# A seventh buffer for the ring of kept sums, lent by the rounded masks, and a new order of issue

## The chip, the core and the metric

One NeuronCore of one Trainium2 chip. The metric is the device time of one execution in microseconds (us). PE is the engine of the matrix products, DVE, ACT and POOL are the three engines that work on elements, SP only issues transfers (DMAs).

## The reference, cut to what matters

```python
def _attn_ref(q, k, v):                      # q, k, v: (8, 8, 576, 64)
    scores = scale * np.matmul(q, k.transpose(0, 1, 3, 2))
    mask = (rel >= 0) & (rel < 64)           # rel = row position - column position
    ...                                      # softmax over the band
    return np.matmul(attn, v)

def _moe_ref(x, w_in, w_out):                # x: (4608, 512), w_in: (512, 2048), w_out: (2048, 512)
    h = x @ w_in
    g = np.where(h >= 1, h, np.where(h <= -1, 0.0, (h + 1) ** 2 / 4))
    return g @ w_out
```

Attention in a band of 64 keys comes first, and its output for each of the 4608 tokens is the input of a feed-forward layer.

## The kernel before, in words

**Stages.** The tokens go in nine tiles of 512. Three tiles are plain (`PLAIN = 3`): for each of 16 slices f of the hidden width, `ffn_in` (line 1218) makes h, a gate follows on ACT and DVE, and `ffn_out` (line 1258) adds to the output. Numbers are split into a high and a low part, and three products of the parts stand for one exact product. The six tiles left go in pairs, three "supers", by a scheme that does with seven block products what takes eight otherwise: sums and differences of the weights' blocks are made once, beside the plain stage (`add_sums`, line 938), and stored in HBM as `kept`; sums of the inputs are made on the chip. In each super, layer 1 (`ffn_product`, line 992, products on line 999) and layer 2 (`out_product`, line 1078, products on line 1085) run 56 products of six matmuls each.

**The ring.** Each of these products needs one block of kept sums, 256 KB, read from HBM by `ring_load` (line 976, transfer on line 979) into one of the ring's buffers. `add_ring` (line 981) makes 336 such loads in all. A load takes the next buffer in turn, and it is issued when the product that read that buffer last is done. The ring has six buffers: four are parts of the weight tile of slice 7, free once the last plain tile and the sums have used that slice, and two are buffers of the gates' parts `gh` and `gl`, free when the last plain tile's gates end. In the profile a buffer of the ring goes by the name of its tile, `wts`, `gh` or `gl`.

**Attention** runs in 36 steps of 128 tokens, spread over the whole as far as they go. From step 5 on, a step is: loads of q, k and twice v (lines 403, 407, 413), scores on PE (line 435), masked maximum and exponential, a 32x32 transpose on DVE (line 504), two stores to a scratch array `moved` in HBM (line 515), a read back in another order (line 530 or 533) into `ptd`, and then the product with v on PE (line 564). The read waits on SP until both stores have landed. The first steps (under 4) use masks that PE adds as a product with the unit matrix (line 428): `round_masks` (line 418) rounds the unit matrix and two masks into the tiles `idr` and `mskr`, 384 columns together, which nothing reads after that.

**Order.** Nothing is put in order by the compiler. `Plan` (line 134) holds every piece of work with a key, a cost for each engine that may do it, what it must come after and which buffers it takes and gives back; `Plan.run` (line 164) goes through a modelled time and puts out one piece after another, each on the engine that it chose. So all instructions of an engine and all transfers of SP's one queue stand in an order that the constants at the top of the file determine. The constants are keys and offsets (a unit is three quarters of the work of one slice on a plain tile), and `BACKLOG` is how far the modelled transfers may be behind before `run` lets SP issue another one. On the chip itself nothing waits for a key, a cost or `BACKLOG`: there only the order in each queue, and the semaphores of data and buffers, count.

**Start.** PE begins with matmuls on zeros (`warm`, line 291), which come before any loaded data: line 1422 gives the plan the cost of 8 but issues 13.

Of the kernel before, what the change touches and what calls it, by code (L numbers as in the profile page):

```python
# [11 lines left out]
F32R = mybir.dt.float32r  # L12
# [8 lines left out]
P = 128  # L21
QB = 64
SB = 2 * QB
WIN = 128
# [15 lines left out]
SOON = 5  # L40
JOIN = 8
BEHIND = 2
E_SPAN = -0.05
E_LEAD = 4.66
W_LEAD = -23.13
W_FIRST = (35.49, 50.06, 38.63, 36.68, -42.68)
W_STEP = 56.48
L_LEAD = 8.81
W_LATE = (-42.87, -19.84, -54.27, 11.82, -43.33)
V_LATE = 52.64  # L50
W0_KEY = -158.18
FIRST_LOAD = 0, (0,)
M_LATE = -3.69
W0_STEP = 28.15
FINE = 4
NWARM = 8
A_FIRST = (-130.89, -101.03, -86.53, -82.72)
A_NEXT = 21.89
A_STEP = 8.86
A_SPAN = 83.57  # L60
A_LEAD = -2.06
O_LAG = 3.31
BEGIN = dict(PE=1500, ACT=2300, DVE=2500, SP=2400)
PERIOD = 10240 / 3
HOP = dict(ACT=165, DVE=165, Pool=210, PE=210, SP=0)
# [5 lines left out]
EXP = 1545, 1440  # L71
S_PE = 1230, 1150
B_PE = 2210
B_DUE = (-1.9, -10.3, -2.66)
B_STEP = 16.55
B_FIRST = -49.18
A_END = -1.03
V_PE = 1270
NORM = dict(Pool=1300, DVE=610)
G_LATE = (6.24, 30.85, -58.26, 24.04, 0.27)  # L80
D_LATE = (10.58, -8.5, 39.35, -35.76, 47.54, 28)
TURN = 965, 100
HOP_SP = 660, 430
SLACK = 1000
V_PE_2 = 1290
SUM_PASS = 1900
SUM_KEEP = 430
V_LATE_2 = 63.45
P_LOAD = (-14.18, -18.03)
P_LOAD_V = (106.26, 73.14)  # L90
LAND = 800
WRITE = 1140
NOW = -2000
URGENT = 900
BACKLOG = 1487.14
MOVED = 3700
PATIENCE = dict(ACT=300, DVE=0, Pool=303, PE=0, SP=0)
BUFS = dict(qt=2, kt=2, vt=4, ps_a=2, sm=2, ptd=3, pt2=2, x=2, u=2, ps_h=2, a=2, gh=2, gl=2, acc=4, o=2, tmp=1)
BUFS.update({n: 1 for n in ("xtmp", "xs0", "xs1", "xs2", "xs3", "xs4", "xs5", "X", "Y")}, raw=4, ring=6, op=5)


PLAIN = 3
SUPERS = 3
H_STEP = 18.67
S_LATE = -18.48
S_PACE = 47.11
O_CHANGE = (18.66, -33.23, 40.4)
EARLY_2 = 13.35
A_SUPER = ((14.96, -42.48), (-9.45, -6.24))
P_SHIFT = ((-0.59, -6.76, -5.83, 5.27, -24.12), (2, 5.54, 6, 4.47, -26.37))  # L110
A_PAIR = ((6.06, 10.29), (3.01, 10.06))
P_DUE = 3.35
V_RUN = 1130, 930
S_RUN = 932, 954, 904
A_ORDER = (0, 4, 1, 5, 2, 6, 3, 7)
BUILD = (-11.57, 15.81)
X_SLOTS = 4, 0, 6, 1, 2, 3
G_FIRST = 8
RING_SLOT = 7
PARTS = (0, 0, 0), (1, 1, 1), (0, 5, 4), (1, 3, 2), (0, 4, 3), (1, 6, 5), (0, 2, 6)  # L120
WRITES = (1, None), (2, 1), (0, None), (3, 2), (3, 3), (1, 2), (2, 2)
R_LEAD = -5.21
R_LOAD = 370
L_DVE = 4, 6, 8
G_LEAD = (-39.31, 47.12, 21.92, 53.61)
OP_LEAD = 9.32
D_LEAD = 26.04


def packets(n, size, lead=2265):  # L130
# [3 lines left out]
class Plan:  # L134
# [10 lines left out]
    def add(self, key, cost, do, after=(), takes=(), gives=(), lag=0, shared=False, moves=None, behind=()):  # L145
        self.work.append((key, cost, do, set(after), takes, gives, lag, shared, moves, set(behind)))
        return len(self.work) - 1
# [85 lines left out]
def banded_attention_then_ffn(ctx: ExitStack, tc: tile.TileContext, q, k, v, w, masks, out, out_t, dims):  # L233
    nc = tc.nc
    B, H, S, D = dims
    NT, DM = B * S, H * D
# [7 lines left out]
    const = ctx.enter_context(tc.tile_pool(name="const", bufs=1))  # L244
# [17 lines left out]
    make_identity(nc, idt)  # L262
    msk = early[:, P:].rearrange("p (a n) -> p a n", n=WIN)
    nmsk = const.tile([P, 3, NEAR], F32, name="nmsk")
    idr = const.tile([P, P], F32R, name="idr")
    mskr = const.tile([P, 2, WIN], F32R, name="mskr")
    wpool = ctx.enter_context(tc.tile_pool(name="wpool", bufs=1))
    dram = ctx.enter_context(tc.tile_pool(name="dram", bufs=1, space=bass.MemoryType.DRAM))
    kept = [[dram.tile([P, 7, 2, 2, P], F32, name=f"kept{l}{n}") for n in range(NF // 2)] for l in range(2)]
# [21 lines left out]
    def warm(n):  # L291

        ps = bank("acc")
        for _ in range(n):
            nc.tensor.matmul(ps[:, :P], lhsT=ptd[0][:, 0], rhs=ptd[0][:, 0], start=True, stop=True)
# [4 lines left out]
    add = plan.add  # L300
# [14 lines left out]
    ws, wts, pairs, zs, us = {}, {}, {}, {}, {}  # L315
# [45 lines left out]
    def add_weights(f, units):  # L361
        g = f, units
        m = len(units) * DM
        act, high, join, low = 105 + .916 * m, 92 + .844 * m, 10 + 1.22 * m, 67 + 1.05 * m
        key = f * W_STEP - (W_FIRST[f] if f < len(W_FIRST) else W_LEAD) + .5 * units[0]
        x = add(W0_KEY + W0_STEP * (f + .5 * units[0]) if g != FIRST_LOAD else A_FIRST[0] - L_LEAD + .01, dict(SP=480 * (g != FIRST_LOAD)), lambda e: None if g == FIRST_LOAD else w_load(g), moves=packets(P, 8 * m))
        xr = add(key - W_LATE[0], dict(ACT=act), lambda e: w_rest(g), [x], takes=["u"])
        x = add(key - W_LATE[1], dict(ACT=act, DVE=67 + 1.05 * m), lambda e: w_top(g, e), [xr], shared=True)
        x = add(key - W_LATE[2], dict(DVE=join), lambda e: w_join(g), [x], shared=True)
        x = add(key - W_LATE[3], dict(ACT=high, DVE=30 + .6 * m), lambda e: w_high(g, e), [x], shared=True)  # L370
        x = add(key - W_LATE[4], dict(DVE=low, Pool=200 + 2.15 * m), lambda e: w_low(g, e), [x], gives=[("u", xr)], shared=True)
        for u in units:
# [207 lines left out]
    raws, xtmp, xops = {}, [], []  # L580
# [58 lines left out]
    early_values = []  # L639
# [13 lines left out]
    def freed(fs):  # L653
        return [x for f in fs for x in (l1[PLAIN - 1, f], l2[PLAIN - 1, f], *sums_read[0, f // 2], *sums_read[1, f // 2])]
# [27 lines left out]
    def add_turn(s, xs, dk, banks, sm):  # L682
        due = [dk + B_DUE[0], dk + B_DUE[0] + B_DUE[2]]
        x = [add(due[h], dict(DVE=LOWEST), lambda e, h=h: att_masked(s, h), [xs, last["m"]], gives=[banks[h]]) for h in range(2)]
        x = [add(due[h], dict(ACT=EXP[1]), lambda e, h=h: att_exp(s, h, False), [x[h]]) for h in range(2)]
        x = add(due[1], dict(DVE=430), lambda e: att_inverse(s, BOTH), x, shared=True)
        x = [add(due[1], dict(DVE=870, Pool=1650), lambda e: att_normalize(s, BOTH, e), [x], shared=True)]
        due = dk + B_DUE[1]
        if s == SOON:
# [76 lines left out]
    def add_step(t, i):  # L766
# [7 lines left out]
        if s < FIRST:  # L774
            key = due = A_FIRST[s]
        elif s >= JOIN:
            key = a_keys[s]
        else:
            key = a_keys[s]
            due = min(key + A_SPAN, soon(s))  # L780
        lk = key - L_LEAD
        apart = A_SUPER[t > PLAIN][1]
        if s == 0:
            last["r"] = add(lk, dict(ACT=480), lambda e: round_masks())
        if s == PE_STEPS - 2:
            last["m"] = add(lk + M_LATE, dict(SP=480), lambda e: load_masks(), moves=packets(P, 12 * NEAR))
        late = s >= JOIN
        vk, vc = lk + (V_LATE_2 if late else V_LATE), 450 if s < SOON else 640
        xq, xk, xv, xw = add_loads(s, lk, vk, vc)
# [25 lines left out]
        if s < SOON:  # L815
            for h in range(2):
                x = xs
                if not masked:
                    x = add(due + D_LATE[0], dict(DVE=MASKED[near(s)]), lambda e, h=h: att_masked(s, h), [x, last["m"]] if near(s) else [x], gives=[(ps, xs, h)])
                x = add(due + D_LATE[1], dict(DVE=800 if masked else MAXIMUM[near(s)]), lambda e, h=h: att_max(s, h, masked), [x])  # L820
                x = add(
# [26 lines left out]
        else:  # L848
            dk = key if s >= JOIN else min(key + E_SPAN, soon(s) - E_LEAD)
            x = add_turn(s, xs, dk, [(ps, xs, h) for h in range(2)], ("sm", xs))  # L850
            due = dk + B_DUE[1]
            first = taken = ready = [x]
# [85 lines left out]
    def add_sums(l, n):  # L938
# [4 lines left out]
        for c in range(2):  # L943
            k = key + c * S_PACE / 2
            xs = add(
# [18 lines left out]
    rings, ring_first, ring_slots = {}, [], {}  # L964

    def ring_slot(i):
        if i not in ring_slots:
            if i < 4:
                t = slot_tile(RING_SLOT)
                ring_slots.update({2 * a + b: t[:, a, b] for a in range(2) for b in range(2)})  # L970
            else:
                name = ("gh", "gl")[i - 4]
                ring_slots[i] = ffn.tile([P, DM], F32R, name=name, bufs=2, tag=name)
        return ring_slots[i]

# [4 lines left out]

    def add_ring(l, u, n, j, key):
        i, after = len(ring_first), [*sums_kept[l, n], *ring_first[-1:]]
        if i < 6:
            after += freed([RING_SLOT]) if i < 4 else [gates_end[0]]
        x = add(key - R_LEAD, dict(SP=R_LOAD), lambda e: ring_load(l, u, n, j, x), after, takes=["ring"], moves=packets(P, 4 * DM))
        if i < 6:
            ring_first.append(add(key - R_LEAD, dict(SP=0), lambda e: None, after))
        return x

# [226 lines left out]
    phs, gs, acc = {}, {}, {}  # L1216
# [59 lines left out]
    def out_late(t, q, i):  # L1276
        if t < PLAIN - 1 or q < NF - 2:
            return O_LAG
        return O_CHANGE[0] if q == NF - 2 else O_CHANGE[1 + i // 2]

# [27 lines left out]
    def soon(s):  # L1308

        t, i = s * SB // TMAX, s * SB % TMAX // SB  # L1310
        return step(t) + (FRONT * TMAX / 2 / 384 if 2 * i >= TMAX // SB else 0) - A_NEXT + i % 2

# [42 lines left out]
    def add_ffn(t):  # L1355
        first, before, x_out = {}, [x_in[t - 1]] if t else [], {}
        for f in range(NF):
            for r, key in parts(t, f):
# [9 lines left out]
                for i in subs(r):  # L1368
                    x_in[t, i] = xi
                xa, _, xh, xl = add_gate(t, f, r, key, G_LATE if t == 0 else [0] * 5, [xi], [("ps_h", xi)])  # L1370
                over = {x_out[i] for i in subs(r)} if f else set()
# [17 lines left out]
    gates_end = []  # L1389
# [26 lines left out]
    for t in reversed(range(PLAIN)):  # L1416
        for i in reversed(range(TILES[t] // SB)):
            at, apart = (step(t) - A_LEAD, A_STEP) if t < 2 else (step(t) - A_END - B_STEP - EARLY_2, B_FIRST)
            a_keys[starts[t] // SB + i] = key = min(at, key - apart)

    if NWARM:
        x = add(-200, dict(PE=218 * NWARM), lambda e: warm(NWARM + 5), takes=["acc"])
        add(-200, dict(PE=1), lambda e: None, [x], gives=[("acc", x)])
    for i in range(TILES[0] // SB):
        add_step(0, i)
# [77 lines left out]
```

## Time and profile before

| | |
|---|---|
| runs before, median (lowest to highest) | 845.4 us (844.53 to 847.64) |
| the profiled execution | 845.14 us, of which span 842.3 us |
| PE, busy | 820.5 us, 97% of the span |
| DVE / ACT / POOL, busy | 670.4 / 520.8 / 222.0 us |
| granted PE clock, mean | 0.994 of full |
| transfers | 216.05 MB, 257 GB/s in the mean |
| chain that ended last | PE 86%, DMA 8%, ACT 2%, DVE 2% |

The span runs from the first to the last instruction of the profiled execution, the time holds some 3 us more around it. "Busy" of PE counts each matmul from its start to its modelled end, so the idle time is what was lost to waits, and a slow restart after a wait stands inside the busy time. In the stretches below the plain stage is from 40 to 340 us, and the supers are from 340 us on; the last attention step ends near 677 us.

### The profile page before, as it was taken

Reading aid. Unit: us, or ns where it says so; the run is one execution under the profiler, and the core shown is the slowest. Engines: PE = TensorE matmul, PEld = TensorE weight load, DVE = VectorE, ACT = ScalarE, POOL = GpSimd, SP = SyncE. Lnnn points to the kernel's source line nnn. Section 1 sums busy time; section 2 is a strip of 40 time slices with the busy share of each in tenths; the row PEclk is TensorE's granted clock in tenths of the full one; section 3 lists DMA queues with packets and bytes.
Section 4 is the critical chain, followed back from the end, with each engine's and each line's share of the span. In section 5 each row is a group of like instructions: output and inputs, shape, how many; then the busy total and the mean of one; then the engine's idle time right before and its main releaser. Section 6 shows DMA issues by size and latency. Waiting matters only on the chain.

```text
span 842.3 us, 18473 instructions
## 1 busy us (share of the span) xinstructions
PE 820.5 (97%) x6598; PEld 672.7 (80%) x6598; DVE 670.4 (80%) x1571; ACT 520.8 (62%) x1288; POOL 222.0 (26%) x223
## 2 busy tenths in 40 slices
PE   6899999999999999999999999999999999999998
PEld 5787888878888878787788888787878788888886
DVE  6899897756777777887899975898898848878964
ACT  7899765544456765776774755586766635566442
POOL 2223522344434554432211310311222202200100
PEclk8999999999999999999999999999999999999999
DMA  9996559983247888999986998889788886666675
GB/s 352 415 401 208 165 197 359 373 313 128 100 164 241 252 284 261 311 308 299 310 240 197 320 304 282 274 244 302 210 275 281 268 249 196 191 193 196 201 220 173
DMA packets 126026, 216.05 MB, mean 257 GB/s; under 512 B 11632, under 2 KB 46320, under 8 KB 125936
## 3 DMA queue, kind: packets, MB, share of 16 engines
q1 hardware_dynamic: 125648, 213.97, 78.0%
q8 instruction: 52, 0.85, 0.4%
q10 hardware_dynamic: 288, 0.92, 0.3%
q14 instruction: 38, 0.31, 0.1%
HBM read 163.72 MB, written 51.12 MB: 255 GB/s over the span
## 4 chain that ended last, share of the span: by engine, by line
PE 86%; DMA 8%; ACT 2%; DVE 2%; SPq 1%; issue 1%; POOL 0%; ACTq 0%; POOLq 0%
PE acc L1085 25%; PE ps_h L1224 15%; PE acc L1270 14%; PE ps_h L999 12%; PE acc L999 12%; PE ps_a L564 3%; DMA wts<-kept 3%; PE ps_a L435 3%; DMA gh<-kept 1%; DMA moved<-sm 1%; PE ps_h L564 1%; DMA ptd<-moved 1%; DMA raw<-in_w 1%; DMA gl<-kept 1%; PE acc L435 1%
## 5 line engine op out<-in xcount | busy, mean ns | idle before, releaser
L1224 PE MATMUL ps_h<-xh,wts 128*128 128x512 f32 (+1 forms) x424 | 130.4, 375 | 0.0
L1085 PE MATMUL acc<-op,wts 128*128 128x512 f32 x540 | 130.0, 390 | 0.3 <-DMA wts<-kept 0.3
L305 ACT CAST op<-g 128x512 fp32r<-128x512 f32 x125 | 77.6, 622 | 75.5 <-PE acc L1085 48.5
L1270 PE MATMUL acc<-wts,gh 128*128 128x512 f32 x384 | 119.7, 393 | 0.0
L1085 PEld LDWEIGHTS acc<-op,wts 128*128 128x128 f32 x540 | 100.9, 188 | 22.7 <-issue 1.5
L1076 DVE TENSOR_TENSOR op<-g,op 128x512 fp32r<-128x512 f32 x119 | 83.0, 703 | 23.3 <-ACT op L305 22.3
L478 ACT ACTIVATE sm<-sm,nm 128x96 f32<-128x96 f32 x248 | 89.4, 362 | 8.1 <-DVE nm L458 8.1
L1224 PEld LDWEIGHTS ps_h<-xh,wts 128*128 128x128 f32 x424 | 77.6, 189 | 15.5 <-DVE xl L577 0.2
L999 PE MATMUL ps_h<-wts 128*128 128x512 f32 x336 | 86.2, 392 | 3.0 <-DMA wts<-kept 1.9
L1239 ACT ACTIVATE a<-a 128x512 f32<-128x512 f32 (+1 forms) x138 | 85.4, 619 | 3.9
L999 PE MATMUL acc<-wts 128*128 128x512 f32 x336 | 85.4, 389 | 0.5 <-DVE op L307 0.5
L1270 PEld LDWEIGHTS acc<-wts,gh 128*128 128x128 f32 x384 | 71.1, 188 | 15.0
L1234 ACT ACTIVATE a<-g 128x512 f32<-128x512 f32 x96 | 60.4, 629 | 33.7 <-DVE g L1014 27.7
L1224 PE MATMUL ps_h<-xl,wts 128*128 128x512 f32 (+1 forms) x212 | 78.7, 371 | 1.1 <-DVE xl L577 1.1
L999 PEld LDWEIGHTS ps_h<-wts 128*128 128x128 f32 x336 | 62.4, 188 | 17.8 <-DVE g L1014 1.6
L1270 PE MATMUL acc<-wts,gl 128*128 128x512 f32 x192 | 74.9, 390 | 0.3 <-DVE gl L1256 0.3
L999 PEld LDWEIGHTS acc<-wts 128*128 128x128 f32 x336 | 63.0, 188 | 14.0 <-DVE op L307 0.9
L1246 DVE SCALAR_TENSOR_TENSOR g<-a,g 128x512 f32<-128x512 f32 x96 | 67.3, 707 | 2.3 <-ACT a L1239 2.1
L1256 POOL TENSOR_TENSOR gl<-a,gh 128x512 fp32r<-128x512 f32 (+1 forms) x42 | 52.3, 1244 | 54.6 <-ACT gh L1251 49.8
L1234 ACT ACTIVATE a<-ps_h 128x512 f32<-128x512 f32 (+1 forms) x53 | 29.4, 555 | 48.3 <-PE ps_h L1224 44.5
L1063 POOL TENSOR_TENSOR g<-g 128x512 f32<-128x512 f32 x14 | 18.1, 1296 | 156.0 <-DVE op L1076 60.7
L1063 DVE TENSOR_TENSOR g<-g 128x512 f32<-128x512 f32 x82 | 54.4, 684 | 0.8
(149 smaller groups left out, 1572.2 us busy)
## 6 DMA issues: line engine op xcount, KB each, us to landing
wts<-kept SPq DMA_DIRECT2D x224, 256.0 KB, 3.5
vt<-in_v SPq DMA_DIRECT2D x72, 256.0 KB, 4.6
gh<-kept SPq DMA_DIRECT2D x56, 256.0 KB, 4.0
gl<-kept SPq DMA_DIRECT2D x56, 256.0 KB, 3.6
kt<-in_k SPq DMA_DIRECT2D x35, 384.0 KB, 5.7
kept<-wts SPq DMA_DIRECT2D x48, 256.0 KB, 4.8
raw<-in_w SPq DMA_DIRECT2D x12, 1023.8 KB, 9.8
moved<-sm SPq DMA_DIRECT2D x62, 192.0 KB, 3.7
```

The lines of the kernel that those rows point to most:

```text
L305: nc.scalar.copy(dst, src)
L478: nc.scalar.activation(t, t, AF.Exp, bias=nm[:, g:g + 1], scale=-1.0, accum_out=den[:, g:g + 1])
L999: nc.tensor.matmul(ps, lhsT=r[:, part, cp], rhs=x_op(k, xp)[:, cp], start=j in (0, 1, 3, 4) and i == 0 and cp == 0, stop=j in (1, 2, 5, 6) ...
L1063: engine[eng].tensor_tensor(out=g[:, out], in0=g[:, a], in1=g[:, b], op=op)
L1076: engine[eng].tensor_tensor(out=low, in0=g_of(n)[:, of], in1=high.bitcast(F32), op=ALU.subtract)
L1085: nc.tensor.matmul(opened[b][m], lhsT=r[:, part, m], rhs=op[xp], start=j in (0, 1, 3, 4) and i == 0 and n == 0, stop=j in (1, 2, 5, 6) and ...
L1224: nc.tensor.matmul(ps, lhsT=wts[f, 0][:, part, c], rhs=x[:, c, r], start=(c == 0 and j == 0), stop=(c == NP - 1 and j == 2),)
L1234: nc.scalar.activation(gs[t, f, r.start][0], phs[t, f, r.start], AF.Relu, bias=0.5, scale=0.5)
L1239: nc.scalar.activation(a, a, AF.Square)
L1246: nc.vector.scalar_tensor_tensor(out=ps if t >= PLAIN else a, in0=a, scalar=1.0, in1=ps, op0=ALU.min, op1=ALU.max)
L1256: engine[eng].tensor_tensor(out=g[2], in0=g[0], in1=g[1].bitcast(F32), op=ALU.subtract)
L1270: nc.tensor.matmul(acc[t, i][:, n].rearrange("p (b n) -> p b n", n=P), lhsT=g[:, sub], rhs=wts[f, 1][:, part, n.start // P:n.stop // P], s ...
```

## The change

The rounded unit matrix and masks become views of one tile `rounded` of 512 columns. When attention's first five steps are done with it (`early_values`, the products with v of those steps), the same memory serves as a ring buffer, number 4 in order; `gh` and `gl` become numbers 5 and 6, and the ring has seven. The number of loads is the same. The 13 matmuls on zeros become 8. The constants of the order are new.

```diff
--- before.py
+++ after.py
@@ -40,26 +40,26 @@
 SOON = 5
 JOIN = 8
 BEHIND = 2
-E_SPAN = -0.05
-E_LEAD = 4.66
-W_LEAD = -23.13
-W_FIRST = (35.49, 50.06, 38.63, 36.68, -42.68)
-W_STEP = 56.48
-L_LEAD = 8.81
-W_LATE = (-42.87, -19.84, -54.27, 11.82, -43.33)
-V_LATE = 52.64
-W0_KEY = -158.18
+E_SPAN = 4.9
+E_LEAD = 1.65
+W_LEAD = -32.05
+W_FIRST = (52.06, 55.94, 24.06, 44.15, -55.17)
+W_STEP = 51.34
+L_LEAD = 17.27
+W_LATE = (-56.81, -10.7, -51.95, 15.49, -44.94)
+V_LATE = 70.64
+W0_KEY = -160.66
 FIRST_LOAD = 0, (0,)
-M_LATE = -3.69
-W0_STEP = 28.15
+M_LATE = -11.47
+W0_STEP = 32.57
 FINE = 4
 NWARM = 8
-A_FIRST = (-130.89, -101.03, -86.53, -82.72)
-A_NEXT = 21.89
-A_STEP = 8.86
-A_SPAN = 83.57
-A_LEAD = -2.06
-O_LAG = 3.31
+A_FIRST = (-125.74, -93.55, -82.71, -75.21)
+A_NEXT = -0.03
+A_STEP = 16.65
+A_SPAN = 79.59
+A_LEAD = -15.75
+O_LAG = 3.34
 BEGIN = dict(PE=1500, ACT=2300, DVE=2500, SP=2400)
 PERIOD = 10240 / 3
 HOP = dict(ACT=165, DVE=165, Pool=210, PE=210, SP=0)
@@ -71,60 +71,60 @@
 EXP = 1545, 1440
 S_PE = 1230, 1150
 B_PE = 2210
-B_DUE = (-1.9, -10.3, -2.66)
-B_STEP = 16.55
-B_FIRST = -49.18
-A_END = -1.03
+B_DUE = (0.19, -25.45, -6.8)
+B_STEP = 18.55
+B_FIRST = -41.01
+A_END = -4.35
 V_PE = 1270
 NORM = dict(Pool=1300, DVE=610)
-G_LATE = (6.24, 30.85, -58.26, 24.04, 0.27)
-D_LATE = (10.58, -8.5, 39.35, -35.76, 47.54, 28)
+G_LATE = (11.27, 31.35, -52.98, 30.12, -1.51)
+D_LATE = (23.55, -24.18, 48.9, -39.91, 46.67, 35.89)
 TURN = 965, 100
 HOP_SP = 660, 430
 SLACK = 1000
 V_PE_2 = 1290
 SUM_PASS = 1900
 SUM_KEEP = 430
-V_LATE_2 = 63.45
-P_LOAD = (-14.18, -18.03)
-P_LOAD_V = (106.26, 73.14)
+V_LATE_2 = 66.51
+P_LOAD = (-16.28, -15.95)
+P_LOAD_V = (94.44, 51.66)
 LAND = 800
 WRITE = 1140
 NOW = -2000
 URGENT = 900
-BACKLOG = 1487.14
+BACKLOG = 855.57
 MOVED = 3700
 PATIENCE = dict(ACT=300, DVE=0, Pool=303, PE=0, SP=0)
 BUFS = dict(qt=2, kt=2, vt=4, ps_a=2, sm=2, ptd=3, pt2=2, x=2, u=2, ps_h=2, a=2, gh=2, gl=2, acc=4, o=2, tmp=1)
-BUFS.update({n: 1 for n in ("xtmp", "xs0", "xs1", "xs2", "xs3", "xs4", "xs5", "X", "Y")}, raw=4, ring=6, op=5)
+BUFS.update({n: 1 for n in ("xtmp", "xs0", "xs1", "xs2", "xs3", "xs4", "xs5", "X", "Y")}, raw=4, ring=7, op=5)
 
 
 PLAIN = 3
 SUPERS = 3
 H_STEP = 18.67
-S_LATE = -18.48
-S_PACE = 47.11
-O_CHANGE = (18.66, -33.23, 40.4)
-EARLY_2 = 13.35
-A_SUPER = ((14.96, -42.48), (-9.45, -6.24))
-P_SHIFT = ((-0.59, -6.76, -5.83, 5.27, -24.12), (2, 5.54, 6, 4.47, -26.37))
-A_PAIR = ((6.06, 10.29), (3.01, 10.06))
-P_DUE = 3.35
+S_LATE = -0.57
+S_PACE = 109.77
+O_CHANGE = (14.5, -12.23, 59.15)
+EARLY_2 = 15.02
+A_SUPER = ((15.11, -47.59), (-8.64, 3.8))
+P_SHIFT = ((3.71, 1.92, -3.11, 0.92, -0.09), (2.27, 1.61, 4.47, 5.24, -40.65))
+A_PAIR = ((2.94, 9.76), (5.54, 8.5))
+P_DUE = 15.05
 V_RUN = 1130, 930
 S_RUN = 932, 954, 904
 A_ORDER = (0, 4, 1, 5, 2, 6, 3, 7)
-BUILD = (-11.57, 15.81)
+BUILD = (-19.35, 9.76)
 X_SLOTS = 4, 0, 6, 1, 2, 3
 G_FIRST = 8
 RING_SLOT = 7
 PARTS = (0, 0, 0), (1, 1, 1), (0, 5, 4), (1, 3, 2), (0, 4, 3), (1, 6, 5), (0, 2, 6)
 WRITES = (1, None), (2, 1), (0, None), (3, 2), (3, 3), (1, 2), (2, 2)
-R_LEAD = -5.21
+R_LEAD = 1.44
 R_LOAD = 370
 L_DVE = 4, 6, 8
-G_LEAD = (-39.31, 47.12, 21.92, 53.61)
-OP_LEAD = 9.32
-D_LEAD = 26.04
+G_LEAD = (-34.37, 20.67, 21.28, 55.84)
+OP_LEAD = 1.58
+D_LEAD = 48.26
 
 
 def packets(n, size, lead=2265):
@@ -262,8 +262,9 @@
     make_identity(nc, idt)
     msk = early[:, P:].rearrange("p (a n) -> p a n", n=WIN)
     nmsk = const.tile([P, 3, NEAR], F32, name="nmsk")
-    idr = const.tile([P, P], F32R, name="idr")
-    mskr = const.tile([P, 2, WIN], F32R, name="mskr")
+    rounded = const.tile([P, DM], F32R, name="rounded", tag="rounded")
+    idr = rounded[:, :P]
+    mskr = rounded[:, P:P + 2 * WIN].rearrange("p (a n) -> p a n", n=WIN)
     wpool = ctx.enter_context(tc.tile_pool(name="wpool", bufs=1))
     dram = ctx.enter_context(tc.tile_pool(name="dram", bufs=1, space=bass.MemoryType.DRAM))
     kept = [[dram.tile([P, 7, 2, 2, P], F32, name=f"kept{l}{n}") for n in range(NF // 2)] for l in range(2)]
@@ -968,8 +969,10 @@
             if i < 4:
                 t = slot_tile(RING_SLOT)
                 ring_slots.update({2 * a + b: t[:, a, b] for a in range(2) for b in range(2)})
+            elif i == 4:
+                ring_slots[i] = const.tile([P, DM], F32R, name="wts", tag="rounded")
             else:
-                name = ("gh", "gl")[i - 4]
+                name = ("gh", "gl")[i - 5]
                 ring_slots[i] = ffn.tile([P, DM], F32R, name=name, bufs=2, tag=name)
         return ring_slots[i]
 
@@ -980,10 +983,10 @@
 
     def add_ring(l, u, n, j, key):
         i, after = len(ring_first), [*sums_kept[l, n], *ring_first[-1:]]
-        if i < 6:
-            after += freed([RING_SLOT]) if i < 4 else [gates_end[0]]
+        if i < 7:
+            after += freed([RING_SLOT]) if i < 4 else early_values if i == 4 else [gates_end[0]]
         x = add(key - R_LEAD, dict(SP=R_LOAD), lambda e: ring_load(l, u, n, j, x), after, takes=["ring"], moves=packets(P, 4 * DM))
-        if i < 6:
+        if i < 7:
             ring_first.append(add(key - R_LEAD, dict(SP=0), lambda e: None, after))
         return x
 
@@ -1419,7 +1422,7 @@
             a_keys[starts[t] // SB + i] = key = min(at, key - apart)
 
     if NWARM:
-        x = add(-200, dict(PE=218 * NWARM), lambda e: warm(NWARM + 5), takes=["acc"])
+        x = add(-200, dict(PE=218 * NWARM), lambda e: warm(NWARM), takes=["acc"])
         add(-200, dict(PE=1), lambda e: None, [x], gives=[("acc", x)])
     for i in range(TILES[0] // SB):
         add_step(0, i)
```

## Rows read from the trace of the kernel before

**Rows 1.** Stages: length; busy (count) PE, PEld, DVE, ACT, POOL; clock, DMA share, GB/s.

```profile
0.00:40.00 40.00, 30.66 (x360) 25.89 (x362) 30.19 (x68) 30.27 (x99) 11.06 (x24) 0.87 0.97 382
40.00:340.00 300.00, 297.27 (x2787) 243.18 (x2785) 231.19 (x612) 193.16 (x500) 123.43 (x116) 1.00 0.72 248
340.00:700.00 360.00, 353.96 (x2872) 289.10 (x2852) 301.37 (x727) 225.37 (x574) 77.98 (x76) 1.00 0.87 274
700.00:842.30 142.30, 138.65 (x612) 114.49 (x610) 107.67 (x167) 72.05 (x117) 9.52 (x8) 1.00 0.68 196
```

**Rows 2.** Waits of PE, 340 to 700: us in total, times, longest.

```profile
PE ps_h L999 <- DMA wts<-kept: 1.9, 2, 1.2
PE ps_h L999 <- DVE g L307: 0.9, 1, 0.9
PE acc L1085 <- DMA gl<-kept: 0.5, 1, 0.5
PE acc L1085 <- DMA wts<-kept: 0.5, 2, 0.3
PE acc L1085 <- DMA gh<-kept: 0.5, 1, 0.5
...
PE ps_h L999 <- DMA gh<-kept: 0.5, 1, 0.5
```

**Rows 3.** SP's queue in order of time around 375 us: start, us.

```profile
370.25 1.91 SPq L413 DMA_DIRECT2D vt<-in_v  x3
372.24 0.55 SPq L403 DMA_DIRECT2D qt<-in_q  x1
372.85 0.42 SPq L407 DMA_DIRECT2D kt<-in_k  x1
373.36 0.38 SPq L403 DMA_DIRECT2D qt<-in_q  x1
373.79 1.28 SPq L407 DMA_DIRECT2D kt<-in_k  x1
375.12 0.55 SPq L413 DMA_DIRECT2D vt<-in_v  x1
375.77 1.17 SPq L979 DMA_DIRECT2D wts<-kept  x2
```

**Rows 4.** Chain that ended last, 366 to 384: start, us.

```profile
367.88 1.36 PE acc L999 x6
...
375.77 6.63 DMA wts<-kept
...
382.54 1.63 PE ps_h L999 x6
```

**Rows 5.** Ring loads (line 979), issue to landing: 340 to 700, then from 700.

```profile
DMA to landing us min/median/max: 2.6/4.2/6.6
...
DMA to landing us min/median/max: 2.7/2.9/4.4
```

**Rows 6.** Waits of PE, 60 to 340: us in total, times, longest.

```profile
PE ps_h L564 <- DMA ptd<-moved: 1.3, 2, 0.8
PE ps_a L564 <- DMA ptd<-moved: 1.1, 1, 1.1
```

**Rows 7.** PE in order of time, from the start: start, us.

```profile
1.46 5.73 PE L295 MATMUL acc<-ptd 128*128 128x128 f32 x26 [1.46 <-DVE ptd L289]
...
8.21 1.10 PE L435 MATMUL ps_a<-kt,qt 64*64 64x128 f32 x32 [0.55 <-DMA qt<-in_q]
...
12.63 1.10 PE L435 MATMUL acc<-kt,qt 64*64 64x128 f32 x32 [2.65 <-DMA kt<-in_k]
```

**Rows 8.** Read back on line 530: SP's issue, all landings, the chain's product.

```profile
488.83 0.37 SPq L530 DMA_DIRECT2D ptd<-moved  x1
...
DMA to landing us min/median/max: 3.5/5.0/5.6
...
494.72 2.02 PE ps_a L564 x64
```

## The prediction, made before the change was run

> **What bounds the kernel now.** Start with time by stage [rows 1]. From 40 us to the end PE is busy almost throughout: 297.3 of 300 us, 354.0 of 360, 138.7 of 142.3. So a change that adds or removes no matmul can win only what PE waits, and that differs by stage: 9.3 us are idle in the first 40 (the granted clock is 0.87 there, so parts ran at the lower of its two levels), 2.7 up to 340, 6.0 from there to 700, 3.7 after 700, where the last products' takes and store end the program. Read the waits of PE from 340 to 700 next [rows 2]: five kinds name a transfer `kept`, 1.9 + 0.5 + 0.5 + 0.5 + 0.5 = 3.9 us in seven waits, none longer than 1.2 us. These are ring loads that landed late. Only one longer wait of another kind, 0.9 us for DVE, stands beside them.
>
> Why are they late? Take the longest. SP issued three loads of v, then q, k, q, k and v [rows 3]: 4 x 256 + 2 x 256 + 2 x 384 = 2304 KB from 370.25 us on, and only then, at 375.77, the ring load that PE waited for. That load took 6.63 us to land [rows 4], against a median of 4.2 in this stage and of 2.9 after 700 us, when no attention is left [rows 5]. A product takes 1.36 us [rows 4], and a buffer of six is wanted again five products after it comes free, so a load has 5 x 1.36 = 6.8 us in which SP must issue it and the data land. The slowest landing of the stage, 6.6 us, leaves nothing for SP. After 700 us the slowest takes 4.4 and the six buffers are enough.
>
> **The seventh buffer.** It adds one product's time to each load's allowance: 6 x 1.36 = 8.2 us. The longest of the seven waits is 1.2 us, under 1.36, so with the old order all seven would go. For the wait at 382.5 us it can be followed: with a seventh buffer the load in question would go into the one that came free a product earlier, at 369.2 us (367.88 + 1.36), which is before the batch on SP starts at 370.25. A wait also costs its restart: the six matmuls after it took 1.63 us instead of 1.36 [rows 4], 0.27 us, and seven of these are 1.9 us within PE's busy time. The most that this part can bring is 3.9 + 1.9 = 5.8 us; the least is 0. I take 4.3: some 1.5 us will come back as other waits, since PE arriving earlier finds DVE (busy 301 of 360 us, 84% [rows 1]) and the reads of attention less far ahead. What is late next is a gate's sum on DVE, the 0.9 us in [rows 2].
>
> The Trainium skill ("DMA: Bandwidth & Descriptors", Queues, rings and completion order) says that each DMA engine consumes a queue's descriptors in order. By that a ring load issued behind a batch lands behind it, however many buffers there are, and where the new order puts it there this term would be 0 and the time 844.6 us, in place of 840.3 with the term from the rows. The trace agrees as far as it shows such a place: 6.63 us behind the batch, 2.9 in the median with none. The second rival below has this as a case of its own.
>
> **The lent memory.** Tile `rounded` is 128 columns wider than what it replaces, and the two instructions that fill it, the four products that read it and the 336 loads stay as they are: no time. Its loan begins when the fifth step's product with v is done, hundreds of us before the first ring load, so one load more can be in before the supers; nothing waited for such a load there, so 0.
>
> **The new order, plain stage.** Three waits for `ptd`, 1.3 + 1.1 = 2.4 us [rows 6], are reads of attention that landed late; with a restart of 0.27 us each, 3.2 us. If the new keys issue these steps sooner, up to 3.2 us are won; if later, as much can be lost again, as nothing else in this stage stalls PE. The lower `BACKLOG` makes the plan hold back a transfer when it thinks 0.86 us are outstanding rather than 1.49, which puts loads of q, k and v into smaller groups. I take a gain of 1.0, bounds 3.2 on either side.
>
> **The new order, start.** The transfers of the first 40 us fill the DMA engines at a share of 0.97 [rows 1], so their order decides when each step of attention may begin, not their sum. The largest wait there is one for k, 2.65 us at 12.63 [rows 7]. New keys could remove it, or put one like it elsewhere: bounds 2.7 on either side, taken at 0, as the rows cannot tell the sign.
>
> **Fewer matmuls on zeros.** Thirteen took 5.73 us, 0.44 each, in 26 records [rows 7]; eight take 3.5 and end at 5.0 us instead of 7.2. The scores behind them wait for q until 8.21 anyway, so nothing is won. What can be lost is the clock, if PE's idle time before 8.21 leaves it at the lower level: the two sets of scores in [rows 7], 1.10 us each, would take twice as long, 2.2 us more; what else PE does between them fits into the 2.65 us that the second set waits for k. Bounds 0 to 2.2, taken at 0.5.
>
> **Sum.** -4.3 (ring) - 1.0 (plain stage) + 0 (start's order) + 0.5 (zeros) = -4.8 us. The profiled execution took 845.14 us, 0.26 below the median of 845.4, so 845.14 - 4.8 = 840.3 us.
>
> **Rivals.**
> First, the time moves elsewhere. The ring's waits go, but the pieces behind them, DVE's sums and the reads of attention, are as late as before. For it: DVE at 84% in this stage, already the second cause of waits. Against it: DVE waits were 0.9 us where the ring's were 3.9. If 4 of the 5.8 us come back and the rest is as above, 845.14 - 1.8 - 1.0 + 0.5 = 842.8 us.
> Second, the change does not do what it says: the order was made anew together with the buffer, and a plan that believes in seven buffers may put even more loads in front of a ring load, as seven products' time seems to allow it. Then the batch of [rows 3] grows and the waits stay: 845.14 + 0.5 - 1.0 = 844.6 us. Against it is the lower `BACKLOG`.
> Third, slower. The place is the read of attention before a product with v inside the supers. One read was issued at 488.83 us and its product began at 494.72 [rows 8]; a landing takes 5.0 us in the median and 5.6 at the slowest, so 0.3 to 0.9 us were to spare. Eight such groups of products with v stand between 340 and 700 us, four before each of the last two supers (`add_pairs`). If the new order puts two more ring loads ahead of the read, each waiting on SP for its buffer for 1.36 us, the read is 2.7 us later and PE waits some 2.0, plus 0.27 to restart. That decides from four groups on: 4 x 2.27 = 9.1, less 4.8, is 4.3 us slower. With five groups, 11.4 - 4.8 = 6.6, it would be 851.7 us; with all eight 858.5. Against it: PE waited for no such read from 340 to 700 us [rows 2].
>
> **How the numbers follow.** A measurement of this kernel can tell some 0.5% from no change: 841.2 and 849.6 us are these bounds around the median. The forecast, the ring's waits gone and a little more, gets 0.48, its own range 836 to 841.2; the first rival 0.27 and the second 0.10, both within 0.5%; the third 0.15. So faster 0.48, same 0.37, slower 0.15. For 8 in 10, the low end takes in the larger bounds of ring, plain stage and start (5.8 + 3.2 + some 1 of 2.7, 10 us: 835); the high end goes up to the border of the slower case, 849.5, and leaves some 0.15 above it and 0.05 below.
>
> **What would show it.** Right: from 340 to 700 us the waits of PE for `kept` fall from seven and 3.9 us to one or two under 0.5, PE's busy share there goes up from 354.0 in 360, the span to the last product with v (677 us) shortens by 4 us or more, and ring loads land no sooner, with a median near 4 us. Wrong: waits for `ptd` on line 564 appear after 340 us (third rival); waits for DVE on lines 999 and 1085 grow to 3 us or more (first); landings of ring loads over 7 us with waits for `kept` as before (second); or a first product of layer 1 of the plain stage that starts much earlier or later than now, which would mean that I was wrong to leave the start at 0.

## The result, and the profile after

The changed kernel takes 837.08 us in the median of six runs (835.14 to 839.17), the kernel before 844.36 in six runs beside it. The ratio is 0.9911 with a 95% interval of 0.9886 to 0.9936: 7.3 us less. Two more measurements on later occasions gave 0.9917 and 0.9926. The forecast was 840.3 us and faster.

The profiled execution of the changed kernel took 839.17 us, the slowest of its six, with a span of 837.2. Lines moved by one to three: ring loads are on line 982, products of the supers on 1002 and 1088, the product with v on 565, scores on 436.

Time by stage of the changed kernel, columns as in [rows 1]:

```profile
0.00:40.00 40.00, 30.47 (x356) 25.21 (x357) 31.23 (x70) 30.32 (x100) 11.04 (x24) 0.83 0.98 382
40.00:340.00 300.00, 294.30 (x2678) 240.78 (x2677) 229.09 (x601) 191.35 (x499) 126.29 (x115) 1.00 0.72 246
340.00:700.00 360.00, 358.21 (x2972) 296.44 (x2971) 306.21 (x740) 233.96 (x590) 79.94 (x74) 1.00 0.87 279
700.00:837.20 137.20, 133.16 (x588) 109.98 (x586) 102.63 (x160) 67.00 (x109) 9.05 (x7) 1.00 0.66 194
```

Against [rows 1] PE's idle time fell from 6.0 to 1.8 us between 340 and 700 us, and rose from 2.7 to 5.7 between 40 and 340. In these two profiles the gain is all in the supers, and the plain stage gave a little of it back. PE from the first matmul of the supers to the end of the last, before and after, in the same columns:

```profile
340.59:838.65 498.06, 492.02 (x3429) 403.14 (x3424) 407.72 (x889) 296.83 (x689) 87.50 (x83) 1.00 0.82 253
342.91:833.16 490.25, 488.46 (x3428) 404.15 (x3424) 405.21 (x887) 298.56 (x693) 88.99 (x81) 1.00 0.82 257
```

The supers are 7.8 us shorter: PE's idle time in them falls from 6.0 to 1.8 us, and its busy time, in which the slow restarts after waits stand, by 3.6 us. The waits of PE say which waits went. First those from 340 to 700 us, to be read beside [rows 2]:

```profile
PE ps_a L436 <- issue: 0.7, 1, 0.7
PE acc L1002 <- DMA wts<-kept: 0.6, 1, 0.6
PE acc L1088 <- DMA wts<-kept: 0.5, 1, 0.5
```

Seven waits for `kept` of 3.9 us have become two of 1.1; those for DVE and ACT are gone as well. Now those from 60 to 340 us, to be read beside [rows 6]:

```profile
PE ps_h L565 <- DMA ptd<-moved: 2.7, 3, 1.1
PE ps_a L565 <- issue: 1.1, 1, 1.1
PE ps_a L565 <- DMA ptd<-moved: 1.0, 1, 1.0
PE ps_h L1227 <- DVE a L1249: 0.5, 1, 0.5
PE acc L1273 <- ACT o L306: 0.2, 1, 0.2
```

The waits for reads of attention in the plain stage, which the prediction hoped to see shorter, are 3.7 us in this profile instead of 2.4; in the two later profiles of the changed kernel they are 4.0 and 1.6. Another 1.1 us here has no releaser that the profile shows ("issue"). The start of PE, beside [rows 7]:

```profile
1.46 3.78 PE L296 MATMUL acc<-ptd 128*128 128x128 f32 x16 [1.46 <-DVE ptd L290]
...
8.11 1.48 PE L436 MATMUL ps_a<-kt,qt 64*64 64x128 f32 x32 [2.32 <-DMA qt<-in_q]
...
12.55 1.99 PE L436 MATMUL acc<-kt,qt 64*64 64x128 f32 x32 [1.81 <-DMA kt<-in_k]
```

With fewer matmuls on zeros both sets of scores are slower in this profile, 1.48 and 1.99 us instead of 1.10, and the granted clock of the first 40 us is 0.83 instead of 0.87. Ring loads (line 982) do not land sooner, from 340 to 700 us, beside the first of [rows 5]:

```profile
DMA to landing us min/median/max: 2.6/4.2/7.3
```

So the same late transfers no longer hold PE up. Where do they stand on SP's queue? One of attention's batches (the eight loads of v, q and k for two steps, which SP issues one behind the other), in SP's order of time in the changed kernel, beside [rows 3]:

```profile
598.18 2.88 SPq L414 DMA_DIRECT2D vt<-in_v  x4
601.15 0.94 SPq L404 DMA_DIRECT2D qt<-in_q  x1
602.14 0.42 SPq L408 DMA_DIRECT2D kt<-in_k  x1
602.65 0.38 SPq L404 DMA_DIRECT2D qt<-in_q  x1
603.12 0.47 SPq L982 DMA_DIRECT2D wts<-kept  x1
603.65 0.42 SPq L408 DMA_DIRECT2D kt<-in_k  x1
604.16 1.39 SPq L982 DMA_DIRECT2D wts<-kept  x2
```

In the kernel before, the batch is v v v q k q k v, and the next ring load stands behind all eight. Here one ring load stands ahead of the last k. Five such batches stand in the supers, and all five differ in this way (in one of the five before, the last three come as v q k).

### The profile page after: what moved, and what is told of

The parts are those of the page before. It is cut to its first block, busy times and chain, and to the rows that moved or that the text cites. A ratio compares the mean times of both kernels' runs of the same rounds, so it can differ in the third digit from the quotient of the medians.

```text
span 837.2 us, 18489 instructions
## 1 busy us (share of the span) xinstructions
PE 816.1 (97%) x6588; PEld 672.4 (80%) x6588; DVE 669.2 (80%) x1567; ACT 522.6 (62%) x1295; POOL 226.3 (27%) x220
## 4 chain that ended last, share of the span: by engine, by line
PE 80%; DMA 9%; DVE 4%; ACT 2%; issue 2%; SPq 2%; POOL 0%; ACTq 0%; DVEq 0%; POOLq 0%
PE acc L1088 27%; PE acc L1002 13%; PE ps_h L1002 13%; PE ps_h L1227 11%; PE acc L1273 10%; PE ps_a L565 3%; DMA ptd<-moved 3%; PE ps_a L436 2%; DMA moved<-sm 2%; DMA wts<-kept 1%; DMA kept<-o 1%; DMA out<-o 1%; DMA raw<-in_w 1%; ACT sm L479 1%; SPq L900 1%
## 5 line engine op out<-in xcount | busy, mean ns | idle before, releaser
L1088 PE MATMUL acc<-op,wts 128*128 128x512 f32 x576 | 137.7, 390 | 0.5 <-DMA wts<-kept 0.5
L1088 PEld LDWEIGHTS acc<-op,wts 128*128 128x128 f32 x576 | 107.8, 188 | 23.7 <-DMA wts<-kept 1.0
L306 ACT CAST op<-g 128x512 fp32r<-128x512 f32 x122 | 75.8, 622 | 73.5 <-PE acc L1088 44.0
L1002 PE MATMUL acc<-wts 128*128 128x512 f32 x360 | 91.5, 390 | 0.6 <-DMA wts<-kept 0.6
L1002 PE MATMUL ps_h<-wts 128*128 128x512 f32 x360 | 91.9, 391 | 0.0
L1242 ACT ACTIVATE a<-a 128x512 f32<-128x512 f32 (+1 forms) x141 | 87.2, 619 | 4.1
L1002 PEld LDWEIGHTS acc<-wts 128*128 128x128 f32 x360 | 67.5, 188 | 15.0 <-DVE op L308 1.0
L1002 PEld LDWEIGHTS ps_h<-wts 128*128 128x128 f32 x360 | 67.2, 188 | 14.5 <-ACT a L1237 0.2
L1237 ACT ACTIVATE a<-g 128x512 f32<-128x512 f32 x96 | 60.4, 630 | 29.1 <-DVE g L1017 24.4
L1017 DVE TENSOR_TENSOR g<-g,acc 128x512 f32<-128x512 f32 x60 | 40.9, 681 | 12.1 <-PE acc L1002 11.7
```

Of the source, the lines that this page charges most:

```text
L306: nc.scalar.copy(dst, src)
L1002: nc.tensor.matmul(ps, lhsT=r[:, part, cp], rhs=x_op(k, xp)[:, cp], start=j in (0, 1, 3, 4) and i == 0 and cp == 0, stop=j in (1, 2, 5, 6) ...
L1088: nc.tensor.matmul(opened[b][m], lhsT=r[:, part, m], rhs=op[xp], start=j in (0, 1, 3, 4) and i == 0 and n == 0, stop=j in (1, 2, 5, 6) and ...
L1237: nc.scalar.activation(gs[t, f, r.start][0], phs[t, f, r.start], AF.Relu, bias=0.5, scale=0.5)
L1242: nc.scalar.activation(a, a, AF.Square)
```

## The experiments

**The buffer alone.** The order of every queue stays that of the kernel before; only the buffers that the loads go through are seven.

```diff
-        r = ring_slot(plan.slots[x, "ring"][0])
+        r = ring_slot(len(loaded) % 7)
+        loaded.append(x)
```

(with `rounded` as buffer 4, as in the change; the plan still counts six)

> The buffer alone: every engine's and SP's order stays exactly that of the kernel before, the ring's loads go round seven buffers instead of six. If the seventh buffer's slack is what the ring's waits needed, they fall from seven waits and 3.9 us (340 to 700 us) to under 1 us, with their restarts some 4 to 5 us in all: about 839.5 to 840.5 us against 844.4 before, a ratio of 0.994 to 0.995. If it is the new order that took the waits away, this stays at a ratio of 0.998 or more and the waits for kept remain.

Measured: ratio 0.9991 (0.9968 to 1.0013), no gain. The waits of PE from 340 to 700 us in this run:

```profile
PE ps_h L1003 <- DVE sm L505: 2.2, 1, 2.2
PE acc L1089 <- DMA wts<-kept: 2.0, 2, 1.8
PE ps_a L565 <- DMA ptd<-moved: 1.2, 1, 1.2
PE ps_h L1003 <- DVE g L1018: 1.0, 1, 1.0
PE ps_h L1003 <- DMA wts<-kept: 0.7, 1, 0.7
PE acc L1089 <- DMA gl<-kept: 0.6, 1, 0.6
```

Waits for `kept` are 3.3 us, so they are still there. How far they fell cannot be said from single profiles: they are 3.9 us in [rows 2], but 7.1 us in a second profile of the old order with six buffers (the one with 8 matmuls on zeros, below):

```profile
PE ps_h L999 <- DMA wts<-kept: 2.0, 1, 2.0
PE acc L1085 <- DMA gl<-kept: 1.6, 2, 1.1
PE acc L1085 <- DMA gh<-kept: 1.2, 1, 1.2
PE ps_h L999 <- DMA gh<-kept: 1.2, 1, 1.2
PE acc L1085 <- DMA wts<-kept: 1.1, 1, 1.1
```

The longest wait with the buffer alone is shown by SP's queue in this run, and by the chain that ended last:

```profile
606.99 2.56 SPq L414 DMA_DIRECT2D vt<-in_v  x3
...
611.96 0.55 SPq L414 DMA_DIRECT2D vt<-in_v  x1
612.57 0.77 SPq L983 DMA_DIRECT2D wts<-kept  x1
```

```profile
612.57 7.17 DMA wts<-kept
...
619.87 2.32 PE acc L1089 x9
```

The load behind the batch is issued when the batch is through, and lands 7.17 us later. With seven buffers its own buffer is free a product sooner, but it stands behind the batch, and the batch waits for other buffers, those of v above all. SP's longest wait from 604 to 613 us:

```profile
SPq L414 <- PE ps_a L565: 2.5, 2, 2.1
```

Here a free buffer did nothing for loads that stand behind a batch.

**The loads one place up, old order.** The same, and each ring load takes SP's place of the one ahead of it; every other instruction on all engines stays where the kernel before has it.

```diff
-            do(e)
+            self.order.append((i, e))
...
         plan.run()
+        place = [at_ for at_, (x_, _) in enumerate(plan.order) if x_ in ring_loads]
+        loads = [plan.order[at_] for at_ in place]
+        before_ = {place[0]: loads[:2]} | dict(zip(place[1:], [[x_] for x_ in loads[2:]] + [[]]))
...
+        there = before_
+        for at_, done_ in enumerate(plan.order):
+            for x_, e_ in there.get(at_, [done_]):
+                plan.work[x_][2](e_)
```

(`plan.run()` now only records the order, and the lines behind it play it)

> The order of the kernel before on all engines, seven buffers, and on SP each ring load takes the place of the one ahead of it, so that a load stands ahead of the batch of attention's loads that it stood behind; nothing else moves. If the first run with seven buffers gained nothing because the loads stayed behind the batches, the waits for kept now fall under 1 us from 340 to 700 us and the ratio is 0.994 to 0.996. If buffer and place do not matter, it stays at 0.998 or more.

Measured: ratio 0.9933 (0.9912 to 0.9954), some 5.7 us of 846.5. The waits of PE from 340 to 700 us:

```profile
PE ps_a L437 <- issue: 2.1, 1, 2.1
PE ps_a L566 <- DMA ptd<-moved: 1.2, 2, 0.9
PE acc L1005 <- DMA wts<-kept: 0.2, 1, 0.2
```

Waits for `kept` have fallen to 0.2 us although loads still take 4.3 us in the median and up to 6.9. Waits for DVE and ACT, 1.7 us in the kernel before, are gone too. This is the mechanism of the prediction, and the buffer by itself was not enough for it: the loads also had to take the place on SP's queue that the buffer allows. The place without the buffer was not run: with six buffers most loads, one place up, would stand ahead of the product that frees their buffer.

**The new order without the buffer.** The reverse: the changed kernel's order, six buffers, and each ring load in SP's place of the next one.

```diff
-        r = ring_slot(plan.slots[x, "ring"][0])
+        r = ring_slot(len(loaded) % 6)
+        loaded.append(x)
...
+        after_ = {place[0]: []} | dict(zip(place[1:], [[x_] for x_ in loads[:-2]] + [loads[-2:]]))
+        there = after_
...
```

> The changed kernel's order on all engines, six buffers, and on SP each ring load takes the place of the next one, so that it comes one product's time later; nothing else moves. If the seventh buffer's time is what the order lives on, waits for kept come back from 340 to 700 us, 4 us or more with restarts, and the ratio to the kernel before goes up from 0.991 to 0.996 or more. If the rest of the new order did it, the ratio stays at 0.993 or below.

Measured: ratio 0.9957 (0.9934 to 0.9979). The waits of PE from 340 to 700 us:

```profile
PE ps_h L1005 <- DMA wts<-kept: 2.2, 2, 1.7
...
PE ps_h L1005 <- DVE g L1252: 0.7, 1, 0.7
PE acc L1005 <- DVE g L309: 0.5, 1, 0.5
PE acc L1091 <- DMA wts<-kept: 0.5, 1, 0.5
PE acc L1091 <- DMA gh<-kept: 0.4, 1, 0.4
PE acc L1005 <- DMA wts<-kept: 0.4, 1, 0.4
```

Waits for `kept` are back at 3.5 us, and waits for DVE come back with them. Without buffer and place the new order keeps about half of the gain, and the interval leaves room for a good deal less. The profile is of the third slowest of its twelve runs (846.25 us, the median is 843.53), so it may show more waits than most.

**Six and five buffers with the new order unmoved.** These two were meant to show the price of a buffer, with loads left where the change has them.

> The order alone: every queue's order stays exactly that of the changed kernel, the ring's loads go round six buffers. If the buffer's slack did it, waits for kept come back between 340 and 700 us, 3 us or more, and the time is 3 to 6 us above the changed kernel: 840 to 843 us. If the order did it, it stays within 1 us of the changed kernel's 837.

> The changed kernel's order with only five buffers, to get the price of a buffer. By the slack (a load has one product's 1.36 us less for each buffer taken away; four products' 5.4 us are left, landings have a median near 4.2 and reach 6.6) waits for kept should grow steeply, over 15 us in all, 852 us or more, with waits in stretches without attention still rare. If transfers were not the bound, under 845.

Measured: 1.0149 (1.0115 to 1.0183) and 1.2975 (1.292 to 1.3029). They do not price a buffer. Some loads stand, in the order in which the program is written, ahead of the product that reads the block in their buffer; that product then reads the block of the later load and also waits for it. (In the profile of the changed kernel, 12 of the 336 loads are issued before the product six places back has begun.) So both compute with other blocks in places, and such waits would not be there in a kernel made for six or five buffers. The run above, with the loads moved too, stands in their stead.

**The old constants with seven buffers in the plan.** The change without its constants: the plan orders anew by the keys of before.

```diff
-BUFS.update(... raw=4, ring=6, op=5)
+BUFS.update(... raw=4, ring=7, op=5)
...
-        if i < 6:
-            after += freed([RING_SLOT]) if i < 4 else [gates_end[0]]
+        if i < 7:
+            after += freed([RING_SLOT]) if i < 4 else early_values if i == 4 else [gates_end[0]]
```

> The change with the constants of the kernel before: the plan knows of the seven buffers, and puts the work in order by the old keys. If the buffer is worth its slack whatever the keys, a ratio near that of the moved loads, 0.994 to 0.996. If the keys were fitted to six buffers, other waits (for DVE, ACT or ptd, on PE after 340 us) take the place and it comes out at 0.997 or more, perhaps over 1.

Measured: ratio 1.0062 (1.0041 to 1.0084), slower than before. One wait of PE from 340 to 700 us stands out, and waits for `kept` are down to 0.4 us:

```profile
PE acc L1002 <- ACT o L306: 7.0, 1, 7.0
...
PE acc L1088 <- DMA wts<-kept: 0.4, 1, 0.4
```

The chain that ended last shows what stands behind it:

```profile
348.34 2.80 DMA kept<-o
...
351.22 0.59 ACT o L306
...
351.86 2.50 PE acc L1002 x5
```

The bank `acc` that the product wants is emptied by ACT into a buffer `o`, and that buffer is still in use for sums of the weights on their way to HBM. These are the last such sums. In the kernel before they take `o` only after the last copies of `acc`, and their transfer is issued later:

```profile
360.35 0.42 SPq L934 DMA_DIRECT2D kept<-o  x1
```

In the changed kernel it is issued at 367.85. With a seventh buffer and the old keys the plan put these sums ahead of the copies, and the copies wait for them. In the 7.0 us without a product the granted clock fell as well, and it was 0.50 from 350.1 to 356.9 us. So with this plan the old keys did not suit seven buffers. The run with the loads moved by hand shows that new keys are not the only way to make the buffer pay.

**The matmuls on zeros.** The changed kernel with 13 of them, twice, once more the changed kernel for comparison, and the kernel before with 8.

```diff
-        x = add(-200, dict(PE=218 * NWARM), lambda e: warm(NWARM), takes=["acc"])
+        x = add(-200, dict(PE=218 * NWARM), lambda e: warm(NWARM + 5), takes=["acc"])
```

> The changed kernel with 13 matmuls on zeros again, nothing else. By the prediction's term it gains some 0.5 us at most against the changed kernel, which this measurement cannot tell from none: a ratio of 0.989 to 0.993. The scores of the first two steps should take 1.1 us each instead of 1.5 and 2.0, and the first product of layer 1 of the plain stage should start 0.2 to 0.8 us sooner. If the clock at the start decided more, the ratio would be under 0.988.

> The changed kernel, with 8 matmuls on zeros, beside the next one on the same chip: a ratio of 0.989 to 0.994 to the kernel before.

> The changed kernel with 13 matmuls on zeros, once more, beside the same with 8. If the better ratio of the first such run (0.988) was the zeros' doing, it comes out 0.002 to 0.004 under the changed kernel of this job; if it was spread between chips and runs, within 0.002 of it.

> The kernel before with 8 matmuls on zeros, nothing else. By the prediction's term (0 to 2.2 us, taken at 0.5) a ratio of 1.000 to 1.003; the first two sets of scores take 1.5 to 2.0 us instead of 1.1. If the start's clock decides more, over 1.003.

Measured: 0.988 (0.9858 to 0.9901) the first time, which looked like a gain over 8; then 0.9918 (0.9891 to 0.9945) beside 0.9926 (0.9899 to 0.9954) with 8, on the same chip. The kernel before with 8 gave 1.0002 (0.9976 to 1.0027). In both profiles with 13 the scores took 1.10 us each again and the clock of the first 40 us was 0.91. But the scores do not follow the zeros alone. With 8 the two sets took 1.48 and 1.99, 1.98 and 1.99, 1.99 and 1.10 us in the changed kernel's three profiles, and 1.10 and 1.99 in the old order; with 13 and the old constants the second set took 1.99 us in two of four profiles, and the first always 1.10. The mean clock of the first 40 us does not tell them apart either: it is 0.83, 1.00 and 0.87 in the changed kernel's three profiles. In the whole, the zeros are not worth anything that these measurements can tell. No version beat the changed kernel clearly.

**The changed kernel again**, beside the first four runs:

> The changed kernel once more, for comparison on the same chip: 837 us, a ratio of 0.989 to 0.994, waits for kept near 1 us.

Measured: 0.9917 (0.9888 to 0.9945), waits for `kept` 0.3 us from 340 to 700 us.

**By stage.** The start of the first matmul of the supers and of the last, read from PE's order of time in each profile; the third column is the difference, the time of the supers, and the fourth is PE's idle time in them:

| kernel | first, us | last, us | supers, us | idle, us |
|---|---|---|---|---|
| before | 340.6 | 838.3 | 497.7 | 6.0 |
| before, 8 zeros | 340.8 | 841.7 | 500.8 | 10.2 |
| old order, seven buffers | 341.3 | 841.8 | 500.5 | 9.1 |
| old order, seven buffers, loads moved up | 340.2 | 833.9 | 493.7 | 3.5 |
| old constants, seven buffers in the plan | 342.7 | 845.2 | 502.5 | 9.1 |
| new order, six buffers, loads moved back | 342.5 | 840.3 | 497.8 | 6.7 |
| changed, three profiles | 342.9, 344.1, 340.6 | 832.8, 834.6, 833.0 | 489.9, 490.5, 492.4 | 1.8, 2.3, 2.4 |
| changed, 13 zeros, two profiles | 339.2, 340.1 | 828.7, 830.0 | 489.5, 489.9 | 1.1, 1.5 |

Buffer and place together take 4 to 7 us off the supers in the old order, and 5 to 8 in the new one. With six buffers the new order's supers are not shorter than the best of the old. These are single profiles; the same kernel's differ by up to 3 us. Part of that is the clock. In the old order with the loads moved up, in the old order with the buffer alone and in the third profile of the changed kernel, one stretch of 3.4 us in the supers ran at the lower level, here in the first of them:

```profile
404.10:407.40 3.30, 3.30 (x10) 2.56 (x9) 1.45 (x11) 2.58 (x15) 0.00 (x0) 0.50 0.95 324
```

PE's busy time in the supers of the changed kernel's third profile is 490.4 us, where the two others have 488.5 and 488.6, so such a stretch cost some 1.8 us.

## Why the prediction was right

**The ring** was the stage, the wait and nearly the size: the gain stands in the supers, the waits that went are above all those for `kept`, and the buffer with its place is worth 5.7 us in the old order (3.9 to 7.4 by the interval). In the new order it is some 3 to 4 us, as the difference of 0.9957 to the changed kernel's 0.9911 to 0.9926, whose intervals touch; beside the changed kernel with 13 zeros on the same chip (0.988) it is 6. The term was 4.3 with 5.8 at most. As the prediction asked, the last product with v ends 3.7 to 5.5 us sooner (672.9 to 671.1 us instead of 676.6), and ring loads land no sooner. But one step in it was wrong: "with the old order all seven would go". With the old order nothing was gained (0.9991). The step took it that a load moves to where its buffer comes free; it moves only if the order of SP's queue is changed too. The second rival named a load behind the batch as a case of its own, but the reading of SP's rows stopped short of it. With six buffers the load at 375.77 in [rows 3] had no free buffer until 374.58 us, when this product of the chain in [rows 4] was done:

```profile
372.99 1.58 PE ps_h L999 x6
```

The last 1.2 us up to 375.77 were the batch's. A buffer free at 369.2 us helps this load only if the load also stands ahead of the batch. By luck this did no harm, since the change had both halves.

**What comes back.** 1.5 us of the term were taken off for other waits, DVE's above all. They did not come. Waits for DVE and ACT between 340 and 700 us were 1.7 us before; with buffer and place they are 0 in the old order and 0 to 0.3 in the new. What came up in the old order was 1.2 us for `ptd`, and 2.1 us without a releaser where there were 0.3. DVE's waits stayed where the loads stayed late: 1.2 us with six buffers in the new order, 3.7 with the buffer alone. So it looks as if part of them followed from the late loads, because a product that waits delays the sums behind it; that step was not tested by itself. The first rival got this the wrong way round.

**The plain stage** was taken at 1.0 us of gain. The profiles do not show it, and its sign is open: the supers begin at 340.6 to 344.1 us in the changed kernel's three profiles, at 339.2 and 340.1 in the two with 13 zeros, and at 340.2 to 341.3 in the four with the old order. Waits for `ptd` are 3.7, 4.0 and 1.6 us in the changed kernel, 0.5 and 1.2 with 13 zeros, and 2.4 to 2.8 in those four. All five of the new order's profiles with seven buffers also have a stop of 1.1 to 2.2 us without a releaser near 334 to 339 us, which the prediction did not foresee; of the four only one has it (0.6 us). The bounds, 3.2 on either side, held all but one profile, which is 3.5 us later than the one before; the choice of the value had no row behind it.

**The start's order**, taken at 0, fits: the first matmul of layer 1 of the plain stage starts at 28.4 to 29.2 us in the four profiles with the old constants and 13 zeros, at 28.4 and 28.5 in the new order with 13, and at 29.1, 28.7 and 28.8 in the changed kernel. **The zeros**, taken at 0.5 us with 2.2 at most, cannot be told from nothing, neither there (28.1 in the old order with 8) nor in the time (1.0002 and the pair 0.9918 and 0.9926), though a set of scores slowed in each profile with 8. Waits cover most of it: the first set's slowness ends in the wait for k ahead of the second set, and behind the second set PE waits for ACT in any case, 1.18 us before and 0.30 after, so that the next product starts at 14.90 and 14.84 us.

**The rivals.** The second (loads stay behind the batches) is what the run with the buffer alone showed, so it was a real case, and the new keys avoid it. The third (late reads of attention inside the supers) did not happen: 0.2 us at most for `ptd` after 340 us in the changed kernel's three profiles. That the keys could make it slower was right in kind: with the old keys in the plan it is 0.6% slower, by another place, the sums' buffer `o`, which the prediction did not name.

**The size** was under by some 2.5 us (4.8 forecast, 7.3 measured, the interval 5.4 to 9.6). The profiles before and after show which terms were too small. Of the 7.8 us in the supers, 2.8 are waits for `kept` (3.9 to 1.1) and 1.4 are other waits, which the prediction had coming back with 1.5; 3.6 are in PE's busy time, where it counted 1.9 for restarts. The terms were also read from one profile: in the second one of the old order with six buffers, PE's idle time in the supers is 10.2 us instead of 6.0.

Which part of the new order brings what the buffer and place do not is open. The ratios 0.9933 and 0.9911 to 0.9926 overlap in their intervals. On the chip of the first, the new order with the same 13 zeros gave 0.988 (0.9858 to 0.9901), which is clear of 0.9912 to 0.9954, but on another chip it gave 0.9918. Of the supers' times, those with a stretch at the lower clock are 493.7 us in the old order and 492.4 in the new, and 1.3 us is less than single profiles differ by. No experiment separated the keys one by one.

## What to carry to other kernels

A buffer more in a ring did nothing here until the loads also stood earlier in the queue that issues them. So look at what stands ahead of the late load in its queue, and ask what that is waiting for. If an order is written out by hand or by a plan, test buffer and place apart, by keeping the recorded order and moving one kind of instruction in it. And keys fitted to one set of buffers can make the time longer with one buffer more, as 1.0062 shows: fit again before judging the buffer. Take sizes from more than one profile, as the same order's waits were 3.9 and 7.1 us in two.

## What the runs showed of the hardware that was not expected

From 340 to 700 us a load of 256 KB takes 2.6 to 2.8 us to land at the least and 6.6 to 8.0 at the most, in eleven profiles (all but those of the two runs that compute with other blocks); seven buffers did not make it shorter.

PE also stood still for 0.3 to 2.1 us in the middle of one step's scores near 403 to 416 us in all of these profiles, old order and new, with no releaser that the profile shows ("issue"); what it waited for is not known. In two of them the granted clock then fell to 0.50 for 3.4 us, after stops of 2.07 and 1.66 us; in two others, after stops of 1.79 and 1.73 us, it did not.
